# Fourteen single moves in a hand-written order of attention and feed-forward steps

## The chip, the cores and the metric

The kernel runs on one core of one Trainium2 chip. The metric is the device time of one execution in microseconds. Five engines work side by side, each through its own queue of instructions in order: TensorE (PE, the matrix multiplications), VectorE (DVE), ScalarE (ACT), GpSimd (POOL) and SyncE (SP), which only issues transfers. An instruction waits until what it reads has been written and what it overwrites has been read; everything behind it on the same queue waits too.

## The reference

Cosine attention over 8 batches of 12 heads, 448 rows of 64 elements each, and then a feed-forward layer with a hard swish, all given and returned in 32 bits:

```python
q_n = q / (np.linalg.norm(q, axis=-1, keepdims=True) + 1e-06)
k_n = k / (np.linalg.norm(k, axis=-1, keepdims=True) + 1e-06)
scores = np.matmul(q_n, k_n.transpose(0, 1, 3, 2)) / tau
scores = scores - np.max(scores, axis=-1, keepdims=True)
attn = np.exp(scores)
attn = attn / (np.sum(attn, axis=-1, keepdims=True) + 1e-09)
x = np.matmul(attn, v)            # heads side by side: [3584, 768]
h = x @ w_in                      # [3584, 2048]
g = h * np.clip(h + 3.0, 0.0, 6.0) / 6.0
out = g @ w_out                   # [3584, 768]
```

## The kernel before

Heads are worked in 48 pairs, six to a batch. The queries or the keys of two pairs together are one item: item j belongs to pairs 2(j//2) and 2(j//2)+1, so items 8 and 9 are those of pairs 8 and 9, items 10 and 11 those of pairs 10 and 11. Eight transfers (`W`) bring the first weight matrix in pieces, two for each four of its sixteen column blocks; four more bring the second.

A step is a short word: an operation, an item, pair or group, and sometimes the engine (`v` DVE, `p` POOL, `a` ACT). These occur here:

- `LQ.j` loads item j (448 KB, one SP transfer, `load_qk`, L197) into one of a ring of raw buffers; it waits until the item that held the buffer before has been normalised. `LV.d` loads the v of pairs 2d and 2d+1 (four SP transfers, L212). `W` issues the next weight piece from POOL (L923).
- `SQ.j` squares an item (L227 on ACT, L229 elsewhere; two numbers say which columns), `RE.j` sums the squares on DVE (L241), `NO.d` takes the inverse norms of two items on ACT by logarithm and exponential (L269 to L276; with `v` its end runs on DVE), `NM.j` multiplies them in (L286). Squares live in two buffers, so `SQ.j` waits for `RE.(j-2)`.
- `TR.j` transposes a normalised item on PE (L332) into a bank of the accumulators; `CQ.i`, `CK.i` and `CS.i` copy a pair's queries or keys out of it (L354, later L382 and L392). From item 14 on `XD.j` transposes by a transfer instead.
- `SC.i.g` multiplies group g of a pair's scores on PE (L435, L432), `EX.i.g` exponentiates it on ACT (L453), `VA.i.g` multiplies with v on PE (L475), `VC.i` casts v (L303, L305), `FI.i` divides by the sum on DVE (L495, L496). `BK`/`CX`, or `XP` and `XB` by transfers, turn the result into the columns that the feed-forward layer reads.
- `U` is one unit of the feed-forward layer on PE (L580: one block of 128 columns of the first matrix; L627 and others: the second). `UA` and `UV` are its following halves on ACT (L589) and DVE (L595), which free its bank.
- `DP.n` and `D.n` are n matrix multiplications of zeros on PE (L935, L930) that compute nothing. They stand in the order of PE like any other.

For the first 18 pairs the order of all steps is written out by hand in the list `PLAN`. `run` goes through it word by word and calls each step's function, which appends its instructions to the queues of its engines. So only the order among steps of one queue matters to the chip: two steps of different engines may change places in the text without any effect. Up to pair 5 the scores use a pair of double banks, afterwards (`OPEN`) a ring of six banks in the order in which PE's steps ask for them. Behind pair 17 a loop takes over, whose order is not changed.

Of the kernel before, what the change touches and what calls it, by code (L numbers as in the profile page):

```python
# [18 lines left out]
ORDER = "111111111111111111111111111111222222"  # L19

PLAN = [
# [38 lines left out]
]  # L60


# [1048 lines left out]
```

## Time and profile before

| | us |
|---|---|
| median of three runs | 403.92 |
| lowest and highest run | 403.89, 404.63 |
| span of the profiled execution (its own time) | 404.4 |
| PE busy | 393.7 |
| DVE, ACT, POOL busy | 288.7, 276.7, 236.7 |

The profiled execution is none of the three runs; its span, from the first to the last instruction, is the only time that there is of it. Its rows give the start from the beginning of the span, the length, the engine, the line of the kernel, the operation, what is written and read with shapes, and a count where rows were merged; a bracket gives how long the engine had idled before and what ended that. Starts of instructions on one engine overlap with the end of the one before by up to a tenth of a microsecond, so what one costs its queue is the distance between starts.

### The profile page before, as it was taken

The numbers are of one execution on the slowest core, as the hardware profiler recorded it, in microseconds if no ns is written. First come the engines' busy times: TensorE is split into PE (matmuls) and PEld (weight loads), VectorE is DVE, ScalarE is ACT, GpSimd is POOL, SyncE is SP. The second block draws the span as 40 slices with busy tenths as digits, with TensorE's granted clock in tenths as the row PEclk, the third lists the DMA queues.
The fourth block names the chain that finished last, engine by engine and source line by source line (L and its number), as shares of the span: only waits on it lengthen the run. The fifth ranks groups of instructions, "written<-read, shape, count | busy, mean of one in ns | idle before, by whom it ended". The sixth has DMA issues, their size and how long they took to land.

```text
span 404.4 us, 9618 instructions
## 1 busy us (share of the span) xinstructions
PE 393.7 (97%) x3689; PEld 234.5 (58%) x3689; DVE 288.7 (71%) x512; ACT 276.7 (68%) x604; POOL 236.7 (59%) x232
## 2 busy tenths in 40 slices
PE   7798999999999999999999999999999999999996
PEld 5566656555665555655555556555565556555564
DVE  5898787878498777777857887587656666655663
ACT  4899989887377687687768768768758755225230
POOL 4799945862744997588486875876664600510070
PEclk9999999999999999999999999999999999999999
DMA  8899999999877748786779659986863523140134
GB/s 285 247 235 243 221 221 213 170 219 202 181 168 179 167 111 209 185 222 129 169 200 194 140 149 163 180 190 136 193 147 76 112 45 63 36 88 20 25 74 99
DMA packets 93166, 63.75 MB, mean 158 GB/s; under 512 B 56128, under 2 KB 93120, under 8 KB 93120
## 3 DMA queue, kind: packets, MB, share of 16 engines
q1 hardware_dynamic: 87408, 56.45, 61.1%
q0 software_dynamic: 5312, 6.29, 9.5%
q8 instruction: 29, 0.48, 0.6%
q10 hardware_dynamic: 400, 0.39, 0.3%
q14 instruction: 17, 0.14, 0.1%
HBM read 45.61 MB, written 11.01 MB: 140 GB/s over the span
## 4 chain that ended last, share of the span: by engine, by line
PE 88%; ACT 4%; DVE 3%; DMA 3%; SPq 1%; issue 0%; DVEq 0%; ACTq 0%
PE M L580 23%; PE M L753 16%; PE PV L475 11%; PE Y L580 6%; PE Z L580 6%; PE M L435 6%; PE Z L753 5%; PE Y L753 4%; PE M L833 3%; PE M L627 3%; ACT at L453 3%; DMA big<-in_q_dram 3%; PE Y L435 1%; PE Z L435 1%; PE Y L833 1%; PE Y L627 1%
## 5 line engine op out<-in xcount | busy, mean ns | idle before, releaser
L453 ACT ACTIVATE at<-M 128x448 bf16<-128x448 f32 x194 | 96.8, 564 | 23.2 <-PE M L435 20.7
L580 PEld LDWEIGHTS <-w_in_sb 128*128 128x128 bf16 x768 | 72.3, 98 | 63.1 <-issue 2.5
L580 PE MATMUL M<-xT,w_in_sb 128*128 128x448 bf16 x504 | 107.4, 352 | 0.1
L286 POOL TENSOR_TENSOR nrm<-big,r 128x896 bf16<-128x896 f32 (+1 forms) x47 | 78.1, 1665 | 14.8 <-issue 4.6
L229 POOL TENSOR_TENSOR big<-big 128x896 f32<-128x896 f32 (+5 forms) x45 | 68.1, 1519 | 14.8 <-DMA big<-in_k_dram 8.2
L589 ACT ACTIVATE u<-M,bias 128x448 bf16<-128x448 f32 x84 | 54.9, 655 | 26.3 <-PE M L580 26.0
L475 PEld LDWEIGHTS <-at 128*128 128x128 bf16 (+1 forms) x1536 | 54.1, 97 | 19.9 <-issue 12.1
L595 DVE SCALAR_TENSOR_TENSOR gT<-u,M 128x448 bf16<-128x448 bf16 x73 | 44.6, 617 | 29.2 <-ACT u L589 28.4
L475 PE MATMUL PV<-vx,at 128*128 128x65 bf16 (+1 forms) x1536 | 62.7, 194 | 0.0
L241 DVE TENSOR_REDUCE n<-big 128x14 f32<-128x896 f32 (+1 forms) x50 | 51.5, 1037 | 0.3 <-ACT big L227 0.2
L392 POOL COPY km<-tT 64x128 bf16<-64x128 bf16 x34 | 14.4, 424 | 61.9 <-PE M L435 25.9
L782 POOL TENSOR_TENSOR big<-big 128x384 f32<-128x384 f32 x11 | 11.8, 1077 | 54.6 <-ACT big L801 54.5
L753 PEld LDWEIGHTS <-gT 128*128 128x128 bf16 x288 | 27.8, 98 | 20.0 <-DVE gT L731 0.6
L753 PE MATMUL M<-w_out_sb,gT 128*128 128x384 bf16 x192 | 35.0, 326 | 0.1
L496 DVE TENSOR_TENSOR on<-PV,rc 128x512 bf16<-128x512 f32 x48 | 33.2, 691 | 1.7
L435 PE MATMUL M<-tT,kz 64*128 64x448 bf16 (+1 forms) x171 | 30.9, 351 | 0.5 <-ACT at L453 0.5
L453 ACT ACTIVATE at<-Y 128x448 bf16<-128x448 f32 x50 | 28.2, 564 | 4.3 <-PE Z L435 4.3
L753 PEld LDWEIGHTS <-gs 128*128 128x128 bf16 x224 | 21.5, 98 | 14.7 <-DVE gs L731 0.3
L453 ACT ACTIVATE at<-Z 128x448 bf16<-128x448 f32 x50 | 28.2, 565 | 2.6 <-PE M L435 2.6
L305 POOL CAST vx<-big 128x512 bf16<-128x512 f32 x39 | 28.2, 728 | 3.1 <-DMA big<-in_v_dram 3.0
L580 PE MATMUL Z<-xT,w_in_sb 128*128 128x448 bf16 x132 | 28.6, 353 | 0.0
L580 PE MATMUL Y<-xT,w_in_sb 128*128 128x448 bf16 x132 | 28.6, 352 | 0.0
(128 smaller groups left out, 574.7 us busy)
## 6 DMA issues: line engine op xcount, KB each, us to landing
big<-in_k_dram SPq DMA_DIRECT2D x24, 448.0 KB, 5.1
big<-in_q_dram SPq DMA_DIRECT2D x24, 448.0 KB, 4.5
out_dram<-o SPq DMA_DIRECT2D x107, 96.0 KB, 2.2
big<-in_v_dram SPq DMA_DIRECT2D x48, 128.0 KB, 4.7
big<-in_v_dram SPq DMA_DIRECT2D x48, 96.0 KB, 4.4
w_in_sb<-in_moe_w_in_dram POOLq DMA_DIRECT2D x8, 384.0 KB, 10.4
w_out_sb<-in_moe_w_out_dram POOLq DMA_DIRECT2D x4, 768.0 KB, 10.8
tT<-nrm SPq DMA_TRANSPOSE x34, 2.8
```

Source lines behind the costliest of these rows:

```text
L229: engines[e].tensor_tensor(out=o, in0=i, in1=i, op=ALU.mult)
L241: nc.vector.tensor_reduce(out=n2_and_r[0][:, d % 2, j % 2, c], in_=sq[:, :, :, :].rearrange("p g c d -> p (g c) d")[:, c, :], axis=AX.X, o ...
L286: engines[e].tensor_tensor(out=nrm[:, :, g, :].rearrange("p c g d -> p g c d"), in0=raw_of[j][:, g, :, :], in1=n2_and_r[4][:, d % 2, j % 2, :]
L305: (engines[e].copy if e == "a" else engines[e].tensor_copy)(out=o, in_=f)
L435: nc.tensor.matmul(o, ks, qt[rows], start=True, stop=True)
L453: nc.scalar.activation(out=o, in_=x, func=AF.Exp, scale=inv_tau)
L475: nc.tensor.matmul(pv_out(j, h), at[rows, n, q_cols(i // HP, j)], vt[rows, 3 + h if name == "M" else 5 * h + int(name[1]), :], start=(name ...
L496: nc.vector.tensor_tensor(out=on[:, :, :, :].rearrange("p j h d -> p h j d"), in0=pv4[:, :, :, 0:D], in1=rc[:, :, :].to_broadcast([128, 2, ...
L580: nc.tensor.matmul(ps[:, 0:S], w_in_sb[:, cc, fc * 128 : (fc + 1) * 128], x[:, cc, 0:S], start=(cc == 0), stop=(cc == CC - 1),)
L589: nc.scalar.activation(out=u[:, :], in_=ps[:, 0:S], func=AF.Relu, bias=half_bias, scale=1.0 / 6.0)
L595: nc.vector.scalar_tensor_tensor(out=g[:, fc, c0 : c0 + S], in0=u[:, :], scalar=1.0, in1=ps[:, 0:S], op0=ALU.min, op1=ALU.mult,)
L753: nc.tensor.matmul(m, lhs[:, c, :], rhs[:, c, c0 : c0 + width], start=(base is None and c == 0), stop=(c == KC - 1), skip_group_check=True,)
```

## The change

Every step stays, on its engine, but for one: the first half of `SQ.17` goes from POOL to ACT. PE's order is the same, instruction by instruction; where the text moves `DP` steps, they move past steps of other engines only. Queue by queue this is what changes:

| queue | before | after |
|---|---|---|
| ACT | SQ.3, NO.0.0 | NO.0.0, SQ.3 |
| ACT | EX.11.3, CK.12 | EX.11.3, SQ.17.a.0.4, CK.12 |
| ACT | EX.14.3, EX.15.0, UA | EX.14.3, UA, EX.15.0 |
| DVE | CQ.2, CQ.3, VC.3, CQ.4, CQ.5, NM.5.v.1, RE.7 | NM.5.v.1, CQ.2, CQ.3, VC.3, CQ.4, CQ.5, RE.7 |
| DVE | CK.8, CS.9, CK.9 | CK.8, CK.9, CS.9 |
| DVE | FI.10, UV, UV, VC.12, FI.11 | FI.10, UV, VC.12, UV, FI.11 |
| POOL | SQ.7, W, W, NM.5.p.0, SQ.8, SQ.9 | SQ.7, W, NM.5.p.0, SQ.8, W, SQ.9 |
| POOL | SQ.10, SQ.11, W, NM.7.p.0, VC.4, VC.5 | SQ.10, NM.7.p.0, VC.4, SQ.11, W, VC.5 |
| POOL | NM.13, NM.12 | NM.12, NM.13 |
| POOL | SQ.17.p.0.4, SQ.17.p.4.3 | SQ.17.p.4.3 |
| SP | LV.0, LQ.8, LV.1, LQ.7 | LV.0, LV.1, LQ.8, LQ.7 |
| SP | LQ.10, LQ.9, LV.2, LQ.11, LV.4 | LQ.10, LQ.11, LQ.9, LV.2, LV.4 |
| SP | LQ.14, XP.6, LQ.16, LV.6, LQ.19 | LQ.14, LV.6, XP.6, LQ.16, LQ.19 |
| SP | XD.19, LQ.23, XP.12, LV.11, XD.18, XP.14, LV.10 | XD.19, XP.12, LV.11, XD.18, XP.14, LQ.23, LV.10 |

On SP the stores of finished units stand between the steps of the last row. The lines of the diff that hold these moves:

```diff
--- before.py
+++ after.py
...
-    "NM.1.v.1 DP.1 SQ.3.a.0.7 DP.1 LQ.4 DP.2 D.2 DP.1 DP.2 NM.1.v.0 LV.0 DP.1 DP.2 NO.0.0.v DP.4 SQ.2.a.0.7 TR.1.Y",
-    "CK.1.a DP.1 DP.1 DP.1 DP.2 RE.3 DP.1 RE.2 NM.0.p.1 CK.0.a SQ.5.a.4.3 DP.2 DP.1 DP.4 DP.1 LQ.8 NM.0.p.0",
-    "SQ.4.v.4.3 SQ.5.a.0.4 NO.1 DP.1 DP.2 SQ.4.p.0.4 LV.1 TR.0.Z DP.3 DP.1 DP.1 NM.3.p LQ.7 NM.2.p.0 CQ.0.v SC.0.0.0",
...
-    "LQ.9 DP.1 SC.0.2.0 SC.0.3.1 TR.3.Y CQ.1.v VC.1.v LV.2 CK.2.v DP.2 DP.2 DP.1 DP.1 VC.2.v EX.0.2 SQ.7.p.0.7 LQ.11",
-    "W EX.0.3 TR.2.Z CQ.2.v SC.1.0.0 EX.1.0 SC.1.1.1 CQ.3.v DP.1 SC.1.2.0 TR.4.Z VC.3.v EX.1.1 EX.1.2 SC.1.3.1 VA.0.0",
-    "CQ.4.v EX.1.3 DP.1 CQ.5.v LV.4 DP.2 LV.3 SQ.6.a.0.7 NM.5.v.1 W DP.1 DP.1 RE.7 SC.2.0.0 RE.6 VA.0.1 NM.5.p.0",
-    "SC.2.1.1 VA.0.2 VA.0.3 SQ.8.p.0.7 EX.2.0 EX.2.1 DP.3 SQ.9.p.0.7 DP.1 SC.2.2.0 FI.0 CK.3.v TR.5.Z SC.2.3.1 EX.2.2",
...
-    "EX.3.2 SC.3.3.1 EX.3.3 VA.2.0 SQ.10.p.0.7 RE.9 SQ.11.p.0.7 W NM.7.p.0 VC.4.p CK.5.v DP.1 VA.2.1 VA.2.2 VA.2.3",
...
-    "VC.8.p CX.4.v SC.7.0 VA.5.3 VC.9.p FI.5 TR.9 SC.7.1 EX.6.3 EX.7.0 SC.7.2 SC.7.3 CK.8.v CS.9.v CK.9.v VA.6.0",
...
-    "CQ.11.v CQ.10.a VA.7.2 VA.7.3 NO.6 U FI.7 NM.13.p XP.6 NM.12.p UV UA UV U UA SC.9.0 SC.9.1 EX.9.0 UV U VA.8.0 UA",
-    "EX.9.1 UV U SC.9.2 LQ.16 UA VC.11.v UV LV.6 UV TR.11 SQ.14.p.0.7 CK.10.v SC.9.3 CS.10.v CS.11.v U LQ.19 VA.8.1",
...
-    "EX.11.1 VA.9.3 FI.9 EX.11.2 U U UA SC.11.3 UA UV EX.11.3 SQ.17.p.0.4 UV TR.13.Y CK.13.v CK.12.a RE.14 U UA",
...
-    "SC.12.1 VA.11.0 UV VA.11.1 VA.11.2 SQ.16.p.0.6 SQ.16.p.6.1 VC.14.p VA.11.3 U VC.12.v BK.10 NM.14.p FI.11 EX.12.0",
...
+    "SQ.0.p.8.6 RE.0.0 RE.0.1 NO.0.1 NM.1.v.1 LQ.4 NM.1.v.0 LV.0 NO.0.0.v SQ.3.a.0.7 SQ.2.a.0.7 DP.1 DP.2 DP.1 DP.1",
...
+    "TR.1.Y CK.1.a RE.3 RE.2 NM.0.p.1 CK.0.a SQ.5.a.4.3 LV.1 LQ.8 NM.0.p.0 SQ.4.v.4.3 SQ.5.a.0.4 NO.1 SQ.4.p.0.4 DP.1",
...
+    "RE.5 LQ.6 EX.0.0 DP.1 DP.1 SC.0.1.1 RE.4 NM.2.v.1 EX.0.1 NO.2 NM.4.p LQ.10 VC.0.v LQ.11 LQ.9 DP.1 DP.1 DP.1 DP.1",
...
+    "DP.1 DP.1 TR.2.Z NM.5.v.1 CQ.2.v SC.1.0.0 EX.1.0 SC.1.1.1 CQ.3.v DP.1 SC.1.2.0 TR.4.Z VC.3.v EX.1.1 EX.1.2",
+    "SC.1.3.1 VA.0.0 CQ.4.v EX.1.3 CQ.5.v LV.4 LV.3 SQ.6.a.0.7 RE.7 DP.1 DP.2 DP.1 DP.1 SC.2.0.0 RE.6 VA.0.1 NM.5.p.0",
+    "SC.2.1.1 VA.0.2 VA.0.3 SQ.8.p.0.7 W EX.2.0 EX.2.1 SQ.9.p.0.7 DP.3 DP.1 SC.2.2.0 FI.0 CK.3.v TR.5.Z SC.2.3.1",
...
+    "EX.3.1 EX.3.2 SC.3.3.1 EX.3.3 VA.2.0 SQ.10.p.0.7 RE.9 NM.7.p.0 VC.4.p SQ.11.p.0.7 W CK.5.v DP.1 VA.2.1 VA.2.2",
...
+    "EX.6.2 VC.8.p CX.4.v SC.7.0 VA.5.3 VC.9.p FI.5 TR.9 SC.7.1 EX.6.3 EX.7.0 SC.7.2 SC.7.3 CK.8.v CK.9.v CS.9.v",
...
+    "CQ.11.v CQ.10.a VA.7.2 VA.7.3 NO.6 U FI.7 LV.6 XP.6 NM.12.p NM.13.p UV UA UV U UA SC.9.0 SC.9.1 EX.9.0 UV U",
...
+    "EX.11.0 EX.11.1 VA.9.3 FI.9 EX.11.2 U U UA SC.11.3 UA UV EX.11.3 SQ.17.a.0.4 UV TR.13.Y CK.13.v CK.12.a RE.14 U",
...
+    "SC.12.1 VA.11.0 VC.12.v UV VA.11.1 VA.11.2 SQ.16.p.0.6 SQ.16.p.6.1 VC.14.p VA.11.3 U BK.10 NM.14.p FI.11 EX.12.0",
...
-    "EX.14.3 XD.17 U SC.15.0 U FI.13 EX.15.0 UA UV UA UV UA U UA VA.14.0 VA.14.1 LQ.22 VA.14.2 UV UV CK.16.v VA.14.3",
+    "EX.14.3 XD.17 U SC.15.0 U FI.13 UA EX.15.0 UV UA UV UA U UA VA.14.0 VA.14.1 LQ.22 VA.14.2 UV UV CK.16.v VA.14.3",
...
-    "WS.1 SC.16.0 SC.16.1 VC.17.p SC.16.2 XD.19 EX.16.0 VA.15.2 VA.15.3 EX.16.1 LQ.23 U NM.18.p U VC.19.p XP.12",
...
-    "SC.17.0 WS.y3 SC.17.1 SC.17.2 VA.16.2 XP.14 EX.17.0 EX.17.1 NO.10 SQ.22.v.0.4 EX.17.2 SQ.22.v.4.3 VA.16.3 LV.10",
...
+    "WS.y3 SC.17.1 SC.17.2 VA.16.2 XP.14 EX.17.0 LQ.23 EX.17.1 NO.10 SQ.22.v.0.4 EX.17.2 SQ.22.v.4.3 VA.16.3 LV.10 U",
```

35 rows, old and new, of the table PLAN are left out of this document.

## The prediction

> **What bounds the kernel now.** I read the page first (its span, and the weight loads with their size and time to landing), then the engines' busy time by stage, then the queues around each moved step.
>
> ```profile
> span 404.4 us, 9618 instructions
> w_in_sb<-in_moe_w_in_dram POOLq DMA_DIRECT2D x8, 384.0 KB, 10.4
> ```
>
> ```profile
> 14.90:37.20 22.30, 20.16 (x284) 13.36 (x284) 21.43 (x46) 21.64 (x39) 21.73 (x19) 1.00 1.09 257
> 20.33:25.95 5.62, 5.62 (x85) 3.66 (x84) 5.41 (x11) 5.59 (x10) 5.48 (x6) 1.00 1.05 268
> 44.00:200.00 156.00, 155.77 (x1508) 90.52 (x1508) 120.86 (x201) 119.16 (x267) 103.75 (x95) 1.00 0.85 184
> ```
>
> The columns are the stretch, its length, then busy time of PE, weight load, DVE, ACT, POOL, and at the end granted clock, DMA share and GB/s. From 44 to 200 us, past the last of the moved steps, PE idles 0.23 us in all: no move there can gain more than that, it can only open a new hole. From 14.9 to 37.2 us the three others are full at once (ACT 21.64, DVE 21.43, POOL 21.73 of 22.30): there a delay of the exponentials on ACT goes straight to the end, since PE, full behind it, can't catch up. Before 14.9 us the kernel waits for its first loads. So I price what the change does to the start of the exponentials and to holes in ACT before 37.2 us.
>
> **The early moves.** These are the rows of DVE, PE, ACT and POOL (start, length, group).
>
> ```profile
> 13.59 0.56 DVE L229 TENSOR_TENSOR big<-big 128x384 f32<-128x384 f32 x1 [1.27 <-DMA big<-in_q_dram]
> 16.35 0.82 DVE L286 TENSOR_TENSOR nrm<-big,r 128x448 bf16<-128x448 f32 x1
> 18.58 0.38 DVE L354 COPY kz<-Y 128x448 bf16<-128x448 bf16 x1
> 18.99 0.69 DVE L303 TENSOR_REDUCE vx<-big 128x512 bf16<-128x512 f32 x1
> 19.60 0.68 DVE L354 COPY tT<-Z 128x448 bf16<-128x448 bf16 x2
> 21.54 0.66 DVE L286 TENSOR_TENSOR nrm<-big,r 128x448 bf16<-128x448 f32 x1
> 22.11 2.07 DVE L241 TENSOR_REDUCE n<-big 128x14 f32<-128x896 f32 x2
> 28.03 1.07 DVE L241 TENSOR_REDUCE n<-big 128x14 f32<-128x896 f32 x1
> ```
>
> ```profile
> 20.33 0.55 PE L332 MATMUL Z<-ident,nrm 128*128 128x128 bf16 x7
> 25.65 0.36 PE L435 MATMUL SC<-tT,kz 64*128 64x448 bf16 x2
> ...
> 43.97 1.24 PE M L580 x6
> ```
>
> ```profile
> 11.88 1.04 ACT L227 ACTIVATE big<-big 128x384 f32<-128x384 f32 x2 [0.27 <-DMA big<-in_k_dram]
> 14.90 0.92 ACT L453 ACTIVATE at<-SC 128x896 bf16<-128x896 f32 x1 [0.99 <-PE SC L435]
> 26.06 0.92 ACT L453 ACTIVATE at<-SC 128x896 bf16<-128x896 f32 x1
> 29.14 0.23 ACT L269 ACTIVATE ln<-n 128x28 f32<-128x28 f32 x1
> 35.57 0.24 ACT L269 ACTIVATE ln<-n 128x28 f32<-128x28 f32 x1
> ```
>
> ```profile
> 15.01 4.61 POOL L286 TENSOR_TENSOR nrm<-big,r 128x896 bf16<-128x896 f32 x3
> 20.03 1.68 POOL L229 TENSOR_TENSOR big<-big 128x896 f32<-128x896 f32 x1 [0.42 <-DMA big<-in_k_dram]
> 21.65 1.52 POOL L923 DMA_DIRECT2D w_in_sb<-in_moe_w_in_dram  x2
> 24.26 3.32 POOL L229 TENSOR_TENSOR big<-big 128x896 f32<-128x896 f32 x2
> 29.18 3.31 POOL L229 TENSOR_TENSOR big<-big 128x896 f32<-128x896 f32 x2
> 33.15 0.95 POOL L286 TENSOR_TENSOR nrm<-big,r 128x448 bf16<-128x448 f32 x1
> 34.03 1.16 POOL L305 CAST vx<-big 128x512 bf16<-128x512 f32 x2
> ```
>
> NO.0.0.v ahead of SQ.3.a. Item 0's roots no longer queue behind a square that waits for a load, so NM.0, TR.0 and PE's filler come about a microsecond sooner. But the copy that feeds the first scores (CQ.0) stays behind SQ.4.v on DVE, which at 13.59 us had idled 1.27 us for the load of item 4. Gain 0; the load is the cover.
>
> NM.5.v.1 ahead of CQ.2. It holds DVE for 22.11 - 21.54 = 0.57 us and now stands at 19.60, so CQ.2 and CQ.3 end at 20.85 and not at 20.28. TR.4 rewrites the bank Z that they read; at 20.33 it started on their heels. From there to 25.95 PE has no hole (5.62 of 5.62 us busy, filler included), so the scores of pair 3 at 25.65 are late by the same amount, and EX.3.0 began at 26.06, just behind their end at 26.01. Nothing on ACT covers it: EX.3.0 waits the whole 0.57 us. Queued behind it on DVE only the copies, VC.3 and CQ.4, CQ.5 move; RE.7 stays at 22.11. What it brings, an earlier TR.5, has no waiter: PE reaches TR.5 later than NM.5 is done either way.
>
> LV.1 ahead of LQ.8. VC.2 at 18.99 starts 0.03 us after the copy before it ended (18.58 + 0.38), where the rows after it overlap by 0.08; up to 0.11 us of that is a wait for LV.1, which now lands sooner. Bounds 0 and -0.11; I take -0.11, because VC.2 alone there has no overlap. Against this stands LQ.8:
>
> ```profile
> 9.74 5.02 SPq L212 DMA_DIRECT2D big<-in_v_dram  x4
> 14.00:16.00 2.00, 1.50 (x12) 0.86 (x12) 2.00 (x4) 1.10 (x2) 2.00 (x2) 1.00 0.36 90
> ```
>
> LV.1's four issues held SP for 5.02 us, mostly waiting, so LQ.8 behind them goes out near 14.2. Its own reader, SQ.8 at 24.26, is far. But LQ.7 and LQ.6 queue behind its 448 KB: at the 257 GB/s of the stage, 1.7 us at most, and nothing if it fills the stretch from 14 to 16 us in which the DMA engines had a share of 0.36. SQ.7 (20.03, just after its load) ends at 21.71 and RE.7 starts at 22.11, so the first 0.4 us are covered; bounds 0 and +1.3. I take 0, nearer to the empty stretch, which is longer than the transfer.
>
> LQ.11 ahead of LQ.9 and LV.2; the second weight piece behind SQ.8. SP now waits for NM.4 (POOL, 15.01 + 4.61 = 19.62) before it issues LQ.11; LQ.9 and the four issues of LV.2 stand behind that wait.
>
> ```profile
> 17.99 0.37 SPq L197 DMA_DIRECT2D big<-in_k_dram  x1
> DMA to landing us min/median/max: 6.8/6.8/6.8
> ```
>
> ```profile
> 21.07 0.54 SPq L197 DMA_DIRECT2D big<-in_k_dram  x1
> DMA to landing us min/median/max: 8.7/8.7/8.7
> ```
>
> The first pair of rows is LQ.9 (17.99), the second LQ.11 (21.07). LQ.9 now goes out at 19.65 + 0.54 = 20.2; with its own 6.8 us it lands at 27.0. On POOL SQ.8 can't start before RE.6 has read its buffer (DVE to 22.11 + 2.07 = 24.18), so a piece moved behind it adds its 0.76 us (1.52 for two) to SQ.9: 25.9 + 0.76 = 26.7. SQ.9 starts at the later, 27.0, ends at 28.7, and RE.9 (1.07 us, at 28.03 before) ends at 29.8. NO.4 on ACT waits for RE.9: it was reached at 29.14, and with EX.3 late by 0.57 - 0.11 = 0.46 us it is reached at 29.60. So 0.2 us of the load shows. Bounds: LQ.9 by 26.7, nothing added; at 8.7 us it lands at 28.9 and ACT waits till 31.7, 2.1 us more. I take 6.8, the same transfer's own time.
>
> NM.7.p.0 and VC.4.p ahead of SQ.11 and the third piece. SQ.11 ended at 29.18 + 3.31 = 32.5; now at 32.5 + 0.76 + 0.95 + 0.58 = 34.8, with the late load 35.1; RE.11 on DVE ends at 35.9 to 36.2, where NO.5 is reached at 35.57 + 0.66 = 36.2. Covered, with nothing to spare. The second and third weight piece are issued 2.6 (0.95 + 1.68) and 1.5 us (0.95 + 0.58) later. At 10.4 us to landing the second arrives near 36, and the first unit, its reader, starts at 43.97; the third is read from the fifth unit on. Hidden by 8 us; without that, PE would wait what is missing.
>
> **The later moves.** Each is set against a row.
>
> ```profile
> 67.64 0.48 ACT L352 COPY kz<-Y 128x384 bf16<-128x384 bf16 x1 [0.53 <-DVE kz L354]
> 93.36 0.54 ACT L453 ACTIVATE at<-Z 128x448 bf16<-128x448 f32 x1 [0.91 <-PE M L435]
> 72.54 0.39 PE L509 MATMUL M<-ident,on 128*128 128x128 bf16 x4
> 53.72 4.05 SPq L533 DMA_TRANSPOSE xT<-on  x1
> 74.69 2.27 PE M L580 x12
> 128.49 0.29 POOL L392 COPY km<-tT 64x128 bf16<-64x128 bf16 x1 [5.24 <-DMA tT<-nrm]
> ```
>
> SQ.17's half on ACT falls into the 0.53 us that ACT idles before 67.64. The UA ahead of EX.15.0 falls into the 0.91 us before 93.36. VC.12 ahead of a UV frees that unit's bank some 0.6 us later, near 71.9; BK.10 takes it at 72.5. LV.6 ahead of XP.6 and LQ.16 puts four issues before a transpose that holds SP for 4.05 us at 53.72; if they cost what LV.1's did, 5 us, it is still 11 us ahead of the units at 74.69, the first that read its columns, and LQ.16's square comes behind 70 us. Without that cover PE would wait for it. NM.12 and NM.13 change places on POOL (1.7 us each, by the first row of POOL); between 44 and 60 us PE shows no wait for either. LQ.23 goes behind XP.12, LV.11, XD.18 and XP.14; its square, SQ.23, may be late on POOL, which idles 5.24 us soon after, before 128.49: that much is covered. CK.9 ahead of CS.9 starts a copy that needs no score matrix of pair 7 where one stood that did: bounds 0 and -0.1, taken -0.06. The rest: 0.
>
> **Sum.** +0.57 - 0.11 + 0.2 - 0.06 = +0.6 us. The profiled execution (span 404.4) would take 405.0; it lies 0.5 above the median of the runs, 403.92, so the forecast is 404.5, which is 0.15% more. About 0.2%, 0.8 us, is what a measurement of this kernel tells from no change.
>
> The moved NM.5.v.1 meets POOL's last normalise (to 19.62). The row at 16.35 shows what such a meeting costs: 0.82 us, where the one at 21.54, beside a DMA issue, took 0.66. The Trainium skill, "SBUF — State Buffer", section "Who interferes with whom", says that a DVE instruction with two SBUF inputs and a GpSimd instruction that reads SBUF exclude each other for the whole instruction. By that rule it would wait to 19.62 and the sum would be at most 0.1 higher, 404.6; the rows agree that both are slowed, not that one is fully blocked.
>
> **Rivals.** Slower: the load of item 9 comes late. One mechanism, at NO.4: from LQ.9's landing at 26.8 us on every further microsecond is one on ACT, and past 27.2 the sum exceeds 0.2%. LQ.11 took 8.7 us from an issue at 21.07, beside two weight pieces at 21.65; LQ.9's new issue is 0.9 us from that. Halfway, 7.7 us, LQ.9 lands at 27.9, SQ.9 ends at 29.6, RE.9 at 30.7: ACT loses 1.1 and not 0.2, the time is 405.4; at 8.7 it is 406.4. Against it: the second piece now comes 3 us later. The Trainium skill, "DMA: Bandwidth & Descriptors", section "Queues, rings and completion order", has each engine alternate between queues by packets; by it the first piece alone would already slow LQ.9 as two did LQ.11, whose row agrees with it as far as one row can.
>
> Faster: the first loads land sooner. With LQ.8 out of the way, items 5 and 4 might land earlier. ACT idles 0.27 us before 11.88 and 0.99 before 14.90; both gone, the exponentials start 1.26 earlier, and NM.4, which holds back LQ.11 and LQ.9, moves with them: -1.26 + 0.46 - 0.06 gives 403.1, and less if LQ.9 lands earlier by as much. For it: DVE's 1.27 us of waiting at 13.59. Against it: LQ.8 was issued after both loads on the same queue.
>
> Nothing shows. The delay at TR.4 is taken up by holes of PE, which had 20.16 of 22.30 us busy from 14.9 to 37.2: 403.9. Against it: the stretch behind TR.4 is the full one.
>
> **From this to the numbers.** Forecast 0.40, its own range 404.2 to 404.9; a quarter of it lies over 404.7 (a late RE.11, the port). The late load 0.28, the early load 0.20, nothing 0.12. Faster 0.20; within 0.2% 0.30 + 0.12 = 0.42; slower 0.10 + 0.28 = 0.38. The range runs from 402.9, just under the early load, to 405.8, past the middle of the late one.
>
> **What would show it.** TR.4 at 20.8 and not at 20.3, EX.3.0 at 26.5; RE.9's end as the releaser of ACT's logarithm near 29.8; the first score still at 14.5; PE without new holes from 44 us on. The prediction is wrong if CQ.0 starts clearly before 14.0 us, if ACT waits at NO.4 for more than half a microsecond, or if PE shows a wait of its own after 60 us (a bank, xT or a weight piece that came late).

## The result and the profile after

The change costs 8.5 us: the median of six runs is 412.8 us (406.73 to 413.95), that of the kernel before beside them 404.25 (403.89 to 404.91). The ratio is 1.0147, interval 1.0105 to 1.019. The ratios here and below leave out a kernel's runs that lie far above its fastest (three of these six), so the median over all runs stands beside them (here it is 1.021 of the one before). The forecast was 404.5, with a range to 405.8.

First the busy times by stage, columns as in the prediction (PE, weight load, DVE, ACT, POOL; then granted clock, DMA share, GB/s).

```profile
14.90:37.20 22.30, 16.89 (x226) 11.22 (x222) 20.38 (x31) 18.54 (x30) 20.96 (x18) 0.92 1.05 260
28.00:30.00 2.00, 1.94 (x33) 1.87 (x32) 1.30 (x3) 0.81 (x4) 2.00 (x2) 0.50 1.16 254
36.00:38.00 2.00, 0.00 (x0) 0.00 (x0) 2.00 (x1) 0.71 (x1) 2.00 (x3) 0.95 1.17 260
38.00:40.00 2.00, 0.38 (x4) 0.48 (x5) 1.97 (x5) 0.00 (x0) 1.75 (x3) 0.50 0.84 238
40.00:42.00 2.00, 2.00 (x28) 1.85 (x26) 1.48 (x4) 1.00 (x4) 1.36 (x1) 0.50 1.04 170
42.00:44.00 2.00, 2.00 (x18) 1.14 (x18) 1.23 (x7) 0.54 (x1) 2.00 (x3) 0.50 1.15 178
44.00:200.00 156.00, 155.74 (x1560) 91.71 (x1559) 119.53 (x207) 121.80 (x273) 98.23 (x91) 1.00 0.79 173
```

ACT, which had 21.64 us of work between 14.9 and 37.2, has 18.54; PE 16.89 and not 20.16. From 36 to 38 us PE does nothing at all, and DVE is "busy" with one instruction. Behind its holes PE's granted clock is 0.50 (from 28 to 30 us and from 38 to 44 us). From 44 to 200 us PE is as full as before. In the chain of work that ended last, two DVE pieces stand out ahead of 44 us:

```profile
23.74 2.14 DVE le L272
33.52 4.91 DVE nrm L286
```

These are the rows of DVE, ACT, PE and POOL around them:

```profile
23.74 2.13 DVE L272 TENSOR_SCALAR le<-nr 128x28 f32<-128x28 f32 x1 [0.15 <-ACT nr L270]
33.44 4.99 DVE L286 TENSOR_TENSOR nrm<-big,r 128x448 bf16<-128x448 f32 x1
```

```profile
12.59 1.73 ACT L453 ACTIVATE at<-SC 128x896 bf16<-128x896 f32 x2
29.04 0.23 ACT L269 ACTIVATE ln<-n 128x28 f32<-128x28 f32 x1 [1.93 <-DVE n L241]
40.59 0.23 ACT L269 ACTIVATE ln<-n 128x28 f32<-128x28 f32 x1 [3.89 <-DVE n L241]
```

```profile
39.62 0.58 PE L509 MATMUL Y<-ident,on 128*128 128x128 bf16 x4 [4.11 <-DVE xT L354]
```

```profile
23.42 0.70 POOL L923 DMA_DIRECT2D w_in_sb<-in_moe_w_in_dram  x1
24.13 1.69 POOL L229 TENSOR_TENSOR big<-big 128x896 f32<-128x896 f32 x1
32.67 0.70 POOL L923 DMA_DIRECT2D w_in_sb<-in_moe_w_in_dram  x1
33.36 0.63 POOL L305 CAST vx<-big 128x512 bf16<-128x512 f32 x1
33.93 1.70 POOL L286 TENSOR_TENSOR nrm<-big,r 128x896 bf16<-128x896 f32 x1
35.57 0.61 POOL L305 CAST vx<-big 128x512 bf16<-128x512 f32 x1
36.14 1.68 POOL L286 TENSOR_TENSOR nrm<-big,r 128x896 bf16<-128x896 f32 x1
37.77 1.35 POOL L923 DMA_DIRECT2D w_in_sb<-in_moe_w_in_dram  x2
```

The same two DVE instructions in the profile before, and the weight piece that POOL issues beside the second:

```profile
25.75 0.23 DVE L272 TENSOR_SCALAR le<-nr 128x28 f32<-128x28 f32 x1
32.38 0.61 DVE L286 TENSOR_TENSOR nrm<-big,r 128x448 bf16<-128x448 f32 x1
32.44 0.69 POOL L923 DMA_DIRECT2D w_in_sb<-in_moe_w_in_dram  x1
```

The addition of `NO.3` on DVE (L272, 28 numbers to a partition) took 0.23 us before and takes 2.13. It starts while POOL issues a weight piece and ends 0.05 us after the square behind that piece (24.13 + 1.69 = 25.82). `NM.7.v.1` (L286) took 0.61 us before and takes 4.99: it starts beside a cast, 0.07 us behind the third weight piece, and ends 0.61 us after the last of four POOL instructions that follow each other without a gap (36.14 + 1.68 = 37.82). No other DVE instruction up to 44 us takes noticeably longer than before; what stands behind them on DVE is late: `RE.9`, for which ACT waits 1.93 us at `NO.4`; `RE.11`, 3.89 us at `NO.5`; and the copies into xT, 4.11 us on PE.

A number of the trace's own needs a word: this execution began its exponentials at 12.59 us and not at 14.90, though no load ahead of that was moved. By their times most executions of the kernel before do so too (below), though neither of its two profiles is one of them.

Where the time goes is read best from the starts of single exponentials, set against the profile before (us, plus is later; the third and fourth column are experiments below: `NM.5.v.1` moved alone, and `NO.0.0.v` moved alone, which behaves like the kernel before):

| start before | after | NM.5.v.1 alone | NO.0.0.v alone |
|---|---|---|---|
| EX.0.0, 14.90 | -2.31 | -0.15 | -2.13 |
| EX.3.0, 26.06 | -2.01 | +0.39 | -2.08 |
| EX.4.0, 30.20 (behind NO.4) | +0.51 | +2.19 | -2.08 |
| EX.4.2, 31.80 | +1.01 | +2.81 | -2.08 |
| EX.6.0, 37.60 (behind NO.5) | +6.45 | +8.11 | -2.07 |
| EX.7.0, 39.31 | +6.65 | +8.40 | -2.07 |

The change loses 0.30, then 2.52, 0.50, 5.44 and 0.20 us, and nothing behind pair 7: the last exponential is late by 6.34.

### The profile page after: what moved, and what is told of

Read it like the earlier page. It is cut to its first block, busy times and chain, and to the rows that moved or that the text cites. A ratio compares the mean times of both kernels' runs of the same rounds, so it can differ in the third digit from the quotient of the medians.

```text
span 410.7 us, 9618 instructions
## 1 busy us (share of the span) xinstructions
PE 396.2 (96%) x3689; PEld 237.0 (58%) x3689; DVE 294.6 (72%) x512; ACT 278.4 (68%) x605; POOL 235.5 (57%) x231
## 4 chain that ended last, share of the span: by engine, by line
PE 93%; DVE 4%; ACT 1%; issue 0%; ACTq 0%; DVEq 0%
PE M L580 23%; PE M L753 16%; PE PV L475 12%; PE Z L580 6%; PE Y L580 6%; PE M L435 6%; PE Z L753 5%; PE Y L753 3%; PE M L833 3%; PE M L627 3%; PE PV L935 3%; PE Y L435 1%; DVE nrm L286 1%; PE Z L435 1%; PE SC L435 1%; PE Y L332 1%
## 5 line engine op out<-in xcount | busy, mean ns | idle before, releaser
L286 POOL TENSOR_TENSOR nrm<-big,r 128x896 bf16<-128x896 f32 (+1 forms) x47 | 78.1, 1667 | 23.4 <-ACT r L276 14.0
L229 POOL TENSOR_TENSOR big<-big 128x896 f32<-128x896 f32 (+5 forms) x44 | 67.8, 1543 | 14.9 <-DVE n L241 5.5
L475 PEld LDWEIGHTS <-at 128*128 128x128 bf16 (+1 forms) x1536 | 55.9, 98 | 21.8 <-issue 13.8
L475 PE MATMUL PV<-vx,at 128*128 128x65 bf16 (+1 forms) x1536 | 64.5, 196 | 1.8 <-DVE on L496 1.8
```

Of the source, the lines that this page charges most:

```text
L229: engines[e].tensor_tensor(out=o, in0=i, in1=i, op=ALU.mult)
L286: engines[e].tensor_tensor(out=nrm[:, :, g, :].rearrange("p c g d -> p g c d"), in0=raw_of[j][:, g, :, :], in1=n2_and_r[4][:, d % 2, j % 2, :]
L475: nc.tensor.matmul(pv_out(j, h), at[rows, n, q_cols(i // HP, j)], vt[rows, 3 + h if name == "M" else 5 * h + int(name[1]), :], start=(name ...
```

## The experiments

Each kernel was timed beside the kernel before on the same chip. Ratios are with their 95% interval; medians and extremes are over all runs.

| kernel | median (range) | before | ratio |
|---|---|---|---|
| only LV.1 | 404.89 (404.18 to 410.88) | 404.38 | 1.0018 (0.9982 to 1.0054) |
| only LQ.11 | 404.40 (403.92 to 407.58) | 404.83 | 0.9989 (0.9962 to 1.0015) |
| only NO.0.0.v | 404.22 (403.80 to 405.63) | 404.83 | 0.9995 (0.9977 to 1.0013) |
| only the later moves | 404.94 (404.10 to 407.19) | 404.38 | 1.0015 (0.9995 to 1.0036) |
| these four together | 404.75 (403.70 to 408.66) | 404.25 | 1.0010 (0.9982 to 1.0037) |
| only POOL's early moves | 407.39 (405.77 to 408.66) | 404.38 | 1.0062 (1.0033 to 1.0091) |
| only NM.5.v.1 | 413.35 (412.49 to 414.93) | 404.83 | 1.0215 (1.0174 to 1.0255) |
| after, POOL's early moves undone | 410.00 (405.60 to 415.43) | 404.38 | 1.0054 (1.0027 to 1.0081) |
| after, NM.5.v.1 undone | 407.69 (405.50 to 409.06) | 404.25 | 1.0062 (1.0032 to 1.0093) |

**The moves that do not show in the time.** `LV.1` ahead of `LQ.8`:

```diff
-... SQ.5.a.4.3 ... LQ.8 NM.0.p.0 ... SQ.4.p.0.4 LV.1 TR.0.Z
+... SQ.5.a.4.3 ... LV.1 LQ.8 NM.0.p.0 ... SQ.4.p.0.4 TR.0.Z
```

> Only LV.1 ahead of LQ.8, all else as before. If this move brings the early first loads of the changed kernel (first exponential at 12.59 us, before at 14.90), it stands near 12.6 here too, and the time falls by up to 2.3 us, to 402, unless a stall of DVE behind POOL eats it. If one slow DMA engine comes and goes by itself, whatever the order, the first exponential is at 14.9 or 12.6 by chance, and the runs scatter by some 2 us. The prediction's step said 0.1 us gained.

`LQ.11` ahead of `LQ.9` and `LV.2`:

```diff
-... LQ.10 ... LQ.9 ... LV.2 ... LQ.11
+... LQ.10 ... LQ.11 LQ.9 ... LV.2
```

> Only LQ.11 ahead of LQ.9 and LV.2. By the prediction's rival, item 9 comes late: RE.9 late, ACT waits at NO.4, 0.2 to 2.1 us more. If this move makes the slow executions of the changed kernel and of the one with POOL's moves undone (412 to 415), some executions here lie 7 us or more above before. If not, all lie within 2.5 us.

`NO.0.0.v` ahead of `SQ.3`:

```diff
-NM.1.v.1 ... SQ.3.a.0.7 ... LV.0 ... NO.0.0.v
+NM.1.v.1 ... LV.0 ... NO.0.0.v SQ.3.a.0.7
```

> Only NO.0.0.v ahead of SQ.3. By the prediction nothing, since the first copy waits for the load of item 4; but where the first loads are on time that cover is gone, and the first exponential can come up to 0.5 us sooner: 0.5 us less to no change. If an earlier start shifts DVE against POOL and so brings the slow executions, some lie 5 us or more above before.

All moves behind pair 5, and then these together with the three above:

```diff
-... XP.6 ... LQ.16 ... LV.6              NM.13.p ... NM.12.p      SQ.17.p.0.4
+... LV.6 XP.6 ... LQ.16 ...              NM.12.p ... NM.13.p      SQ.17.a.0.4
-CS.9.v CK.9.v     UV ... UV ... VC.12.v     EX.15.0 UA     XD.19 ... LQ.23 ... XP.14
+CK.9.v CS.9.v     UV ... VC.12.v UV         UA EX.15.0     XD.19 ... XP.14 ... LQ.23
```

> Only the moves behind pair 5 (LV.6, LQ.23, NM.12, SQ.17, CK.9, VC.12, UA); up to 40 us the program is that of before. The changed kernel kept a lag of 6.3 to 6.7 us from pair 6 to the end, so these moves should be worth nothing: within 0.3 us of before. First exponential at 14.90 as before, unless the slow DMA engine comes and goes by itself.

> All of the change but NM.5.v.1 and POOL's early moves: NO.0.0.v, LV.1, LQ.11 and the later moves. Each of them alone lay within 0.2% of before. If there is nothing between them, 403.8 to 404.9 and no execution over 410; a gain of up to 0.5 us from NO.0.0.v is possible.

Each interval holds 1.0, and so does that of all together. Two of the ten runs with `LV.1` alone lie at 409.5 and 410.9; no profile shows them. With `LQ.11` alone, `LQ.9` is issued at 20.13 and lands at 25.73, and `SQ.9` starts at 25.86, where it did before: in this execution the late load of the prediction's first rival does not happen.

The profile of the four together is of one of their two longest runs (407.61 us), and shows a cost that the medians do not. The first exponential is as late as in the profile before (14.73), and ahead of the first scores PE stands for 2.46 us and not 1.05:

```profile
14.33 0.37 PE L435 MATMUL SC<-tT,kz 64*128 64x448 bf16 x2 [2.46 <-DVE tT L354]
16.00:18.00 2.00, 2.00 (x14) 0.93 (x12) 2.00 (x5) 1.84 (x6) 2.00 (x3) 0.50 1.02 385
```

Its granted clock then is 0.50, and the first exponential of pair 1 waits 1.50 us for PE. That fits `NO.0.0.v`, which brings PE's filler sooner, in an execution with late first loads; it was not tried alone in such a one.

**The kernel before once more.**

> The kernel before, unchanged, for a second profile. Every time measured so far lies 1.8 us above the span of the same execution, so the profile of before that the prediction was made from (span 404.4) belongs to a time near 406.2, and the median of before (404.4) to a span near 402.6. If the late first loads of that profile (one DMA engine behind from 6.6 us on) are an accident of that execution, this profile most likely shows the first exponential near 12.6 us and a span near 402.5. If they belong to the kernel, 14.9 and 404.4 come again.

It took 406.03 us with a span of 404.2, and began its exponentials at 14.54: the profile before came again. But in every execution the time lies 1.7 to 2.1 us above its own span (412.47 and 410.7 for the change). So the profile that the prediction started from, span 404.4, is of an execution of some 406.2 us, and the median of before belongs to a span near 402.5. Which of the two a profile shows is not set by what was moved: with only `NO.0.0.v` moved the first exponential starts at 12.76, with only POOL's early moves at 12.17, and with only the later moves at 14.90, though SP's queue up to there is the same in all three. The traces show what is late: a load lands in sixteen parts, and of item 4, for which DVE waits before the first copy, fifteen parts are in by 10.44 us in the profile before and the last comes at 13.49. With only `NO.0.0.v` moved the last part is 0.57 us behind the others, with only POOL's early moves 0.06. Why one part lags in some executions was not tried.

Of the 107 runs of the kernel before that stand beside the experiments one took 412.77 us, as long as those of the changed kernel. No profile shows it, so it is open whether the old order falls into the same waits now and then.

**NM.5.v.1 alone.**

```diff
-CQ.2.v ... CQ.3.v ... VC.3.v ... CQ.4.v ... CQ.5.v ... SQ.6.a.0.7 NM.5.v.1 W ... RE.7
+NM.5.v.1 CQ.2.v ... CQ.3.v ... VC.3.v ... CQ.4.v ... CQ.5.v ... SQ.6.a.0.7 W ... RE.7
```

> Only NM.5.v.1 ahead of CQ.2. By the prediction 0.57 us more. By the theory that a DVE instruction with two operands in SBUF can wait behind POOL: it now stands beside POOL's last normalise, which costs up to 1.7 us in the executions where the copies wait for it, and takes away the wait of 1.4 to 1.5 us that it showed in its old place beside SQ.7 where the first loads were on time; so between 1 us less and 2 us more. Not 8 us in any case, unless it moves a later DVE instruction into POOL's train.

This one move costs 8.7 us (1.0215 of 404.8), and all four runs lie at 412.5 or above: the last clause of the expectation is what happened. Rows of DVE, ACT and POOL of this kernel:

```profile
26.13 1.41 DVE L272 TENSOR_SCALAR le<-nr 128x28 f32<-128x28 f32 x1 [0.15 <-ACT nr L270]
35.24 4.85 DVE L286 TENSOR_TENSOR nrm<-big,r 128x448 bf16<-128x448 f32 x1
```

```profile
21.61 0.54 ACT L453 ACTIVATE at<-SC 128x448 bf16<-128x448 f32 x1 [0.22 <-PE SC L432]
24.81 0.92 ACT L453 ACTIVATE at<-SC 128x896 bf16<-128x896 f32 x1 [0.20 <-PE SC L435]
30.71 0.23 ACT L269 ACTIVATE ln<-n 128x28 f32<-128x28 f32 x1 [1.21 <-DVE n L241]
42.26 0.23 ACT L269 ACTIVATE ln<-n 128x28 f32<-128x28 f32 x1 [3.75 <-DVE n L241]
```

```profile
24.19 3.32 POOL L229 TENSOR_TENSOR big<-big 128x896 f32<-128x896 f32 x2 [0.17 <-DVE n L241]
32.89 0.70 POOL L923 DMA_DIRECT2D w_in_sb<-in_moe_w_in_dram  x1
33.60 0.95 POOL L286 TENSOR_TENSOR nrm<-big,r 128x448 bf16<-128x448 f32 x1
34.48 1.16 POOL L305 CAST vx<-big 128x512 bf16<-128x512 f32 x2
35.61 1.68 POOL L286 TENSOR_TENSOR nrm<-big,r 128x896 bf16<-128x896 f32 x1
37.24 0.60 POOL L305 CAST vx<-big 128x512 bf16<-128x512 f32 x1
37.81 1.68 POOL L286 TENSOR_TENSOR nrm<-big,r 128x896 bf16<-128x896 f32 x1
39.44 1.35 POOL L923 DMA_DIRECT2D w_in_sb<-in_moe_w_in_dram  x2
```

This execution began like the profile before (first exponential 0.15 earlier), so the steps can be read off one by one. The exponentials of pair 3 are late by 0.39 + 0.15 = 0.54 us: the copies of the prediction, at their price, though ACT pays it sooner, at `EX.1.3` and `EX.2.2` (the rows at 21.61 and 24.81), whose scores stand behind `TR.4` too. The addition of `NO.3` starts at 26.13 and not at 25.75. In the profile before it came at the end of `SQ.8` and slipped in ahead of `SQ.9`; here `SQ.9` has begun at 25.83, and the addition ends as that ends, at 27.5. So ACT, which was never idle at `NO.4`, waits 1.21 us there, and pair 4 is late by 2.19. `NM.7.v.1` then comes at 35.24. Before, it began at 32.38, 0.06 us ahead of the third weight piece, and POOL's next product came 0.7 us later; now that piece is long over, and it waits 4.24 us, to the end of POOL's run at 39.49.

**POOL's early moves alone, and without them.** The second weight piece behind `SQ.8`, `NM.7.p.0` and `VC.4` ahead of `SQ.11` and the third piece:

```diff
-SQ.7.p.0.7 ... W ... W ... NM.5.p.0 ... SQ.8.p.0.7 ... SQ.9.p.0.7
+SQ.7.p.0.7 ... W ... NM.5.p.0 ... SQ.8.p.0.7 W ... SQ.9.p.0.7
-SQ.10.p.0.7 RE.9 SQ.11.p.0.7 W NM.7.p.0 VC.4.p
+SQ.10.p.0.7 RE.9 NM.7.p.0 VC.4.p SQ.11.p.0.7 W
```

> Only POOL's early moves on the kernel before: the second weight piece behind SQ.8, NM.7.p.0 and VC.4 ahead of SQ.11 and the third piece. If these moves bring the stalls, NO.3's addition on DVE (0.22 us before) or NM.7.v.1 (0.62 us before) takes 2 to 5 us here, and the time rises by 2 to 7 us. If the stalls need the earlier loads as well, both stay under 1 us and the time is that of before within 1 us (up to 0.6 us for NO.5, which then waits for the later RE.11).

They cost 0.6%, 2.5 us. The rows of DVE and POOL show the same meeting, smaller:

```profile
30.89 2.27 DVE L286 TENSOR_TENSOR nrm<-big,r 128x448 bf16<-128x448 f32 x1
```

```profile
30.40 0.60 POOL L305 CAST vx<-big 128x512 bf16<-128x512 f32 x1
30.97 1.67 POOL L229 TENSOR_TENSOR big<-big 128x896 f32<-128x896 f32 x1
32.59 0.70 POOL L923 DMA_DIRECT2D w_in_sb<-in_moe_w_in_dram  x1
```

The third piece is no longer where `NM.7.v.1` comes. `NM.7.v.1` begins 0.11 us before the end of a cast, does not get in there, and waits for the square that took the place, 1.66 us. The runs fall into two kinds (405.8 to 406.8 and 408.0 to 408.7); the profile is of the shorter, and what the longer ones lose is not seen. With these moves undone in the changed kernel (the same lines, the other way round):

> The changed kernel with POOL's early moves undone, so that POOL's order up to pair 5 is that of before. If POOL's order places the DVE instructions badly, both stalls (2.13 us at NO.3's addition, 4.99 us at NM.7.v.1) go, the lead of 2.3 us at the first exponential stays, and the time is 402 to 403. If they depend on the early start alone, at least one stays and the time is over 405.

It was neither: five runs of 405.6 to 408.2 and five of 411.8 to 415.4. The profile is of a short one, with both DVE instructions under 0.8 us. Since `NM.5.v.1` alone gives times over 412, POOL's moves are not what the long waits need; in company with the other moves of the change the long waits seem to come in some executions and not in others, but no profile shows a long one of this kernel. With `NM.5.v.1` put back behind `CQ.5` and POOL's moves kept:

> The changed kernel with NM.5.v.1 back behind CQ.5. If this move and POOL's early moves make up the whole result, what is left is POOL's: 406 to 409, as POOL's moves alone gave (405.8 to 408.7). If LV.1, LQ.11 or NO.0.0.v matter in company, it lies outside.

The excess of POOL's moves alone is left, and no run is over 409.1: the rest of the change adds nothing to it. The costs do not add up, 8.7 and 2.5 us apart and 8.5 together.

**Are the waits the cause?** Four kernels have the move of `NM.5.v.1` and treat the two DVE instructions, two treat them in the changed kernel.

| kernel | median (range) | before | ratio |
|---|---|---|---|
| NM.5.v.1; NO.3 ends on ACT | 412.00 (411.18 to 414.11) | 404.25 | 1.0193 (1.0153 to 1.0234) |
| NM.5.v.1; NM.7 whole on POOL | 406.15 (405.43 to 408.67) | 404.59 | 1.0035 (1.0012 to 1.0057) |
| NM.5.v.1; both | 404.96 (404.07 to 406.95) | 404.59 | 1.0012 (0.9989 to 1.0035) |
| NM.5.v.1; weight pieces moved | 410.45 (405.40 to 414.20) | 404.25 | 1.0033 (1.0004 to 1.0062) |
| after; NM.7 whole on POOL | 408.11 (407.57 to 410.07) | 404.59 | 1.0090 (1.0059 to 1.0121) |
| after; both | 406.67 (404.24 to 408.86) | 404.28 | 1.0055 (1.0024 to 1.0086) |

The edits are single words of the order:

```diff
-... NO.3.v ...
+... NO.3 ...
-... NM.7.p.0 ... NM.7.v.1 ...
+... NM.7.p ...
-SQ.11.p.0.7 W NM.7.p.0 VC.4.p ... VC.5.p ... NM.9.p W W VC.7.p
+SQ.11.p.0.7 NM.7.p.0 VC.4.p ... VC.5.p W W ... NM.9.p W VC.7.p
```

> NM.5.v.1 ahead of CQ.2, and NO.3 ends on ACT instead of DVE (0.55 us more on ACT, and no addition on DVE at 26.1 us that waits 1.24 us for POOL's square). If the small delay of 0.39 us costs 8 us only because two DVE instructions fall into POOL's train one after the other, the first of the two is gone here: RE.9 is on time, NO.4 is late by 0.4 to 1.0 us. NM.7.v.1 then comes 0.4 to 1.0 us later than its 32.4: if that still meets the weight piece that POOL issues from 32.4 to 33.1, the time is 405 to 406; if it misses it and runs into POOL's casts, it waits to the next weight piece (39.0) all the same and the time is 411 or more. If the cost lies elsewhere (the copies, the bank of TR.4), the time stays near 413.

> NM.5.v.1 ahead of CQ.2, and NM.7 whole on POOL (0.73 us more there), so that no DVE instruction is left that could wait 4 to 6 us behind POOL at 35 us. If that wait is what makes 5 of the 8 to 9 us, the lag at pair 6 falls from 8 us to 2.5 to 4 us, and all executions lie between 404.5 and 409. If the time stays at 412 or more, the wait was only an effect of something else that is late.

> As the one before, and NO.3 ends on ACT, so that neither of the two DVE instructions that waited for POOL is there. What is left of NM.5.v.1's move is what the prediction priced (0.4 to 0.6 us), 0.55 us more on ACT for NO.3, and up to 0.7 us for POOL: 404.5 to 406.5, and no execution over 408.

> NM.5.v.1 ahead of CQ.2, and two weight pieces moved on POOL to the place behind VC.5 (34.9 to 36.3 us), where NM.7.v.1 begins at 35.24; no DVE, ACT or PE instruction is moved. If NM.7.v.1 waits 4.24 us because POOL reads SBUF without a gap, it now takes 0.6 to 0.8 us, ACT's wait at NO.5 (3.75 us) shrinks under 1 us, and the time is 406.5 to 409, some 5 us under that with the same move and the old places. If the wait has another cause, it stays over 3 us and the time near 413.

> The changed kernel with NM.7 whole on POOL. The wait of 4.99 us at NM.7.v.1 is gone, that of NO.3's addition (2.13 us) stays where it comes: 406 to 409, against 412 to 414 with it. If the time stays there, the wait was no cause.

> The changed kernel with NM.7 whole on POOL and NO.3 ended on ACT, so that both DVE instructions that waited for POOL are gone. If the two waits are the whole cost of the change, it is within 1.5 us of before (404.5 to 406). If POOL's early moves cost something of their own beside the waits (RE.11 late for NO.5), 406 to 408.

Without the addition on DVE, `NM.7.v.1` still comes 0.26 us behind the third piece (31.69 against 31.43) and takes 6.25 us: one wait less buys nothing where the other grows.

```profile
31.69 6.25 DVE L286 TENSOR_TENSOR nrm<-big,r 128x448 bf16<-128x448 f32 x1
```

Without `NM.7.v.1` on DVE some 7 of the 8.7 us are gone, and without both the rest, to within the measurement. Rows of ACT, first with `NM.7` on POOL, then with both:

```profile
28.64 0.23 ACT L269 ACTIVATE ln<-n 128x28 f32<-128x28 f32 x1 [1.21 <-DVE n L241]
36.36 0.24 ACT L269 ACTIVATE ln<-n 128x28 f32<-128x28 f32 x1
```

```profile
30.07 0.26 ACT L269 ACTIVATE ln<-n 128x28 f32<-128x28 f32 x1
36.63 0.24 ACT L269 ACTIVATE ln<-n 128x28 f32<-128x28 f32 x1
```

ACT waits at `NO.4` only while the addition is on DVE, and nowhere at `NO.5` (3.75 us with the move alone). So the two waits are the cost of the move. The same two edits were not tried on the kernel before, but its profiles show neither wait, and so nothing there that they could take away. In the changed kernel the same two edits take 6 of 8.5 us; 2.4 are left. What POOL's moves cost beside the two instructions (the runs spread from 404.2 to 408.9) stays open.

Moving two weight pieces to 34.9 us, where `NM.7.v.1` had begun, was to give it a place. By their times five runs have it (405.4 to 407.8) and five don't (413.1 to 414.2). In the profile, one of the long ones, `NM.7.v.1` begins at 33.32 in the midst of the first piece (32.93 to 33.63), and all the same waits until 38.19:

```profile
33.32 5.36 DVE L286 TENSOR_TENSOR nrm<-big,r 128x448 bf16<-128x448 f32 x1
32.93 1.35 POOL L923 DMA_DIRECT2D w_in_sb<-in_moe_w_in_dram  x2
```

In this execution a weight piece under way was no place to come in.

**Single meetings.** Two kernels are the one before with a tail behind its last unit, 24 trials each. In a trial POOL runs a train without gaps (P a product of 128x896, C a cast, W the issue of a weight piece), and DVE after a set delay one product like `NM.7.v.1`, which takes 0.62 us alone.

```diff
+def meet(train, cols):
+    nc.vector.tensor_copy(...)           # waits for the train before
+    nc.gpsimd.tensor_tensor(...)         # waits for that copy
+    for x in train:
+        {"P": product, "C": cast, "W": piece}[x]()
+    for n in cols:
+        nc.vector.tensor_reduce(...)     # the delay: n sums of 64
+    nc.vector.tensor_tensor(out=nrms[0][:, :, 0, :], in0=raws[3][:, 0, :, :], ...)
```

> The kernel before, with a tail of 24 short trials behind its last unit, which only adds time (about 200 us). In each, POOL runs a train without a gap (four products; six casts; products and casts mixed; a weight piece and products), and DVE, after a delay of 0.3 to 1.5 us, one product of 128x448 with both operands in SBUF, which takes 0.62 us alone. If DVE gets its turn at the next end of a POOL instruction, it takes at most 2.3 us beside any train. If it loses its turn to the train as a whole, it takes what is left of the train plus 0.6 us, up to 7 us. If casts are what shuts it out, the first holds in the train of products alone, the second in those with casts.

> The kernel before with a second tail of 24 trials, which only adds time. Twelve have a copy from PSUM directly ahead of DVE's product, as NM.7.v.1 and NM.5.v.1 have in their old places; twelve begin during or behind a weight piece, without the copy. If the copy ahead makes DVE lose its turn, the product waits out the whole train (4 to 7 us) in the trials with the copy and products or casts, where the trials without a copy waited for one instruction (0.75 to 1.84 us). If only a weight piece does it, the first nine take 2.3 us at most, and all that begin while a weight piece is being issued take 5 us or more.

| train | product takes | it ends behind |
|---|---|---|
| PPPP, 6 trials that begin beside a P | 0.92 to 1.94 us | the P that was running |
| CCCCCC, 6 beside a C | 0.68 to 1.01 | the C that was running |
| PCPCP and PCCPCP, 9 beside a P | 0.92 to 1.88 | the P that was running |
| PWPP, 7 beside the first P | 0.72 to 1.84 | that P, ahead of or with the W |
| WPPP, 9 beside the W or the first P | 5.02 to 6.00 | the whole train |
| WCPCP, 2 that begin beside the W | 0.62 and 0.94 | nothing, and the W |
| WCPCP, 2 behind the W | 2.05 and 2.51 | the first P (the one that begins beside the C passes its end) |

DVE's and POOL's rows of one trial with PPPP and one with WPPP, with the same delay:

```profile
416.60 1.50 DVE L1108 TENSOR_TENSOR nrm<-big,r 128x448 bf16<-128x448 f32 x1
...
518.78 5.81 DVE L1108 TENSOR_TENSOR nrm<-big,r 128x448 bf16<-128x448 f32 x1
```

```profile
415.94 6.97 POOL L1085 TENSOR_TENSOR big<-big 128x896 f32<-128x896 f32 x4
...
518.44 0.69 POOL L1097 DMA_DIRECT2D w_in_sb<-in_moe_w_in_dram  x1 [0.27 <-issue]
519.15 4.95 POOL L1085 TENSOR_TENSOR big<-big 128x896 f32<-128x896 f32 x3
```

In the seven trials that are not in the table the product begins within 0.07 us of the train's first instruction, once 0.01 us after the start of a weight piece, and takes 0.61 or 0.62 us.

Without a weight piece neither casts nor the copy ahead of the product (in the first twelve trials of the second tail) make a difference: both expectations about them fall. There the product takes its turn at the next end; behind a weight piece and products alone it passes two or three ends of products and gets in only when POOL stops. No trial without a piece has the product begin beside a cast that a product of POOL follows, as `NM.7.v.1` did with POOL's early moves.

## Why the prediction was wrong

- **NM.5.v.1 ahead of CQ.2** ("Nothing on ACT covers it: EX.3.0 waits the whole 0.57 us") was right in size: `EX.3.0` is 0.54 us late (ACT had waited for it at `EX.1.3` and `EX.2.2`), and the time is 0.4 us longer once the two DVE instructions are out of the way, in an interval that also holds 0. The error is what followed: the step ended at `EX.3.0`, and the same delay was not carried on to what DVE does next. So the sum has +0.57 us for a move that costs 8.7. At `NO.3`'s addition and at `NM.7.v.1` it meant 1.80 and 5.30 us, and 0.62 and 0.29 us in the exponentials just behind them, where ACT waited for PE, whose granted clock was 0.50 to 0.77 there.
- **The port** was weighed for the moved instruction alone, at 0.1 us. The rule of the Trainium skill that I cited there ("SBUF — State Buffer", section "Who interferes with whom": the one that comes second is fully blocked) was put aside because two rows showed 0.05 and 0.21 us. Those rows were meetings near the end of a POOL instruction (0.34 and 0.17 us ahead of it; the second began beside `SQ.7`, which ran until 21.71, and not only beside a DMA issue); the trials with PPPP agree with the rule, 0.92 to 1.94 us, up to the end of the running instruction. Behind a weight piece the wait is longer than the one instruction that the rule speaks of, 5.0 to 6.0 us, and there the measurement decides.
- **POOL's moves** were priced at 0, "covered, with nothing to spare", by the time at which `RE.11` and the weights are wanted. They cost 2.5 us, 1.66 of them seen as a longer `NM.7.v.1`. What was not asked is what the weight pieces were good for where they stood: in all ten profiles in which `NM.7.v.1` took under 0.8 us (two of them with a tail), it began 0.00 to 0.25 us ahead of one.
- **The base.** "It lies 0.5 above the median" compared a span with times. By time it was an execution some 2 us over the median (406.2 against 404.25), with late first loads; the early first loads of the rival named "Faster" are, by the times, what the kernel before mostly has, and no gain of the change.
- **The late load** had too high a price: with `LQ.11` moved alone 5.6 us to landing and not 6.8 to 8.7, and nothing of its 0.2 us at `NO.4`.
- Not contradicted are the zero of `NO.0.0.v` in the median, the 0.06 us of the later moves and the 0.1 us of `LV.1`: intervals of 0.2 to 0.4% (0.7 to 1.5 us) can't tell them from nothing. "PE without new holes from 44 us on" held; PE's holes came ahead of it. `RE.9`'s end did release ACT's logarithm, at 29.04, but after a wait of 1.93 us. Of the three signs that I had named for being wrong two showed: more than half a microsecond of waiting at `NO.4`, which is the failure, and a `CQ.0` clearly before 14.0 us (11.74), which came of the early first loads and not of the change.

## What to carry to other kernels

Where DVE and POOL both work in SBUF, follow a delay to the next DVE instructions that can wait for POOL (here products with two SBUF operands and a small addition), and look at what POOL does at their new starts; an order that works may do so because a DMA issue of POOL happens to stand there, and then a delay of half a microsecond can cost nearly 9, as here. Ask of every instruction that is moved what its neighbours on another engine had from its place, also where nobody waits for its result. And compare the profiled execution with the runs by time, or by span, not one with the other.

## What the runs showed of the hardware

- A DVE product that began 0.15 us or more into a weight piece (a DMA issued by POOL) with a train of POOL products behind it waited for the whole train in nine trials of nine, 5.0 to 6.0 us, even where it began 0.4 us after the piece; without the piece, 21 of 21 waited for one instruction only. Not settled is why: with a cast right behind the piece four trials of four got in sooner (0.62 to 2.51 us), in the kernels casts stood in the trains that were waited out, and there two pieces in a row let DVE in at the end of the first in three profiles (1.20 to 1.29 us) and not in a fourth (5.36). With `NM.5.v.1` alone the piece had ended 1.65 us before `NM.7.v.1` began, longer than in any trial, so that the piece made that wait is not shown.
- The wait also strikes a DVE instruction with one operand, the addition of 28 numbers to a partition: 2.13 us behind a weight piece, and 1.41 us beside a square with no piece directly ahead of it (`NM.5.v.1` alone).
- After a hole of 4.11 us PE's granted clock was 0.50 from 38 to 44 us, while it was busy from 40 on. The Trainium skill ("TensorE: Matmul & The Clock Gate", section "What's actually happening") has half the clock after an idle stretch, released by activity; the trace agrees. The idle stretch that the section names is one window of about 3.4 us; here shorter holes were enough, 1.77 us ahead of 28 us in the same profile and 2.46 us in that of the four moves together, and the measurement decides.
